# Phi exponentials kept in their attention phase, splits on GpSimd, a TensorE warm-up and a separately normalised last group in a four-segment attention and GeGLU kernel

One core of one Trainium2 chip. The metric is the device time of one execution in microseconds (us).

TensorE multiplies matrices; VectorE, ScalarE and GpSimd work element by element; DMA moves data between memories. "Half clock" means that TensorE's matmuls start half as often as they can: 0.425 us apart instead of 0.216 for 512 columns in the kernel before. "pv" is the product p @ vs; "rows" are the inverted denominators of the softmax or the memory, laid out for a matmul that spreads them.

## The reference, cut to what matters

x is 2048 x 448, bf16. It is layer-normalised once; a memory-augmented attention and a GeGLU feed-forward block both read the result, and the output is x + attention * silu(ffn).

```python
for s in range(4):                       # segments of L = 512 rows, 16 heads of 28
    p = softmax(qs @ ks.T * scale + causal_mask)
    a_dot = p @ vs
    pq = phi(qs)                         # phi(t) = t + 1 if t > 0 else exp(t)
    a_mem = (pq @ M) / (pq @ z + 1e-6)
    o = g * a_mem + (1 - g) * a_dot      # g = sigmoid(beta)
    pk = phi(ks)
    M, z = M + pk.T @ vs, z + pk.sum(0)
attn = o @ wo
ffn = (gelu(xn @ w_gate) * (xn @ w_up)) @ w_down     # 448 -> 1792 -> 448
out = x + attn * silu(ffn)
```

## The kernel before

The program is one hand-ordered stream: projections of segment 0, gate/up 0, attention 0, gate/up 1, attention 1, gate/up 2 and 3, attention 2, attention 3, the end. During attention, TensorE gets other matmuls ("filler": projections of the next segment, down projections, output projections) between the scores. During gate/up, leftovers run at numbered steps of a table. `later(n, fn)` puts work off by n ticks; one tick comes per gate/up step and per half step of attention.

The parts that matter, with cuts marked by `# ...`:

```python
pkp = pool("pkp", 2)                                  # buffers of pkT
def phi(g, nm, dst):
    # ...
    nc.scalar.activation(out=e[:], in_=dst[:, g, :], func=ACT.Exp)
    ph = pqT[s][:, g, :] if nm == "wq" else pkp.tile([P, L], BF16, name="pkT")[:]
    def rest():                                       # three VectorE operations
        # ...
        if nm == "wk":
            nc.sync.dma_start_transpose(out=pk[...], in_=ph)   # pkT -> pkb by DMA
    later(1, rest)
# after a projection of q or k:  later(2, lambda: phi(g, nm, dst))

def invert(s, side):                                  # 1/denominators as three bf16 terms
    d = dc.pop((s, side))
    # ... tensor_scalar, reciprocal on VectorE
    for i in range(3):
        nc.vector.tensor_copy(out=t[:, i, :], in_=d[:])
        if i < 2:
            nc.vector.tensor_tensor(out=d[:], in0=d[:], in1=t[:, i, :], op=ALU.subtract)
        nc.sync.dma_start(out=rows[side][...], in_=t[:, i, :])
# combine(s, g): a matmul spreads rows over group g's partitions (m<-rows,spread),
#   then VectorE multiplies and adds into oT; the output projection reads oT

# attention(s, fill): 12 steps (4 groups x 3 blocks), pv two steps behind the scores
while fill and done < 1.5:
    c, f = fill.pop(0); f(); done += c
for k, (g, bk) in enumerate(steps):
    pts[k] = scores(s, g, bk)                         # then exp on ScalarE, mask on GpSimd
    if k >= 2:
        give(k - 2)                                   # pv
    # ... filler by share of the work, tick()

# the end
for f in ends: f()                                    # the last two pv
tick()
for n, u in enumerate(d3[2:]):                        # 18 units of down projection
    run([u])
    if n == 4: invert(3, 0)
    if n >= 8 and n % 2 == 0 and n < 16: combine(3, (n - 8) // 2)
run(finish_units(3))                                  # output projection, product, store
```

## Time and profile before

| | before |
|---|---|
| time, median (lowest to highest) | 304.43 us (303.82 to 304.52) |
| span of the profiled run | 302.1 us |
| TensorE busy | 254.0 us, 84% |
| VectorE, ScalarE, GpSimd busy | 193.8, 156.6, 88.9 us |

TensorE is the bound, so its timeline is the one to cut into phases. I cut it at the first gate/up matmul of each segment, at the first V projection after gate/up 0, at the first memory read of each attention (`m<-pqT,mbd`), at the first q projection after gate/up 3, and at the end of the last output projection of attention 3; the rest is "the end".

### The profile page before, as it was taken

The page shows a single profiled execution, that of the slowest core. Times are in us where ns is not written, and L with a number is a line of the kernel's source. Part 1 is how long each engine was busy: PE and PEld are TensorE (multiplying, and loading weights), DVE is VectorE, ACT ScalarE, POOL GpSimd, SP SyncE. Part 2 cuts the span into 40 slices and gives each one's busy share as a digit, 9 for nine tenths or more (in the row PEclk, how much of TensorE's full clock was granted, in tenths as well). Part 3 has the DMA queues.
Part 4 walks back from the last instruction along what each step waited for, and adds up shares of the span by engine and source line. Part 5 has one row for each costly group of instructions (what it writes and reads, how often), then busy time and mean ns, then how long its engine had stood idle before and what let it go on. Part 6 is the DMA issues. An engine that isn't in the chain of part 4 may idle for free. (4 is left out here: it accounts for less than half of the span.)

```text
span 302.1 us, 4379 instructions
## 1 busy us (share of the span) xinstructions
PE 254.0 (84%) x1530; PEld 109.7 (36%) x1552; DVE 193.8 (64%) x409; ACT 156.6 (52%) x219; POOL 88.9 (29%) x180
## 2 busy tenths in 40 slices
PE   0497999899996895989997899999799878897690
PEld 0243444434433342534342344444333333332240
DVE  6646854547759666579786855665565739942584
ACT  2434473779992334476876233332788767580010
POOL 4100100245412000654650133020177824286000
PEclk9999999999999999799999999999999999997897
DMA  8996023001101232001110220000200001001002
GB/s 237 355 325 119 8 49 81 3 0 21 21 17 21 42 96 65 2 24 33 37 34 1 43 52 0 7 4 3 61 17 17 34 7 16 0 29 39 8 1 69
DMA packets 26358, 15.10 MB, mean 50 GB/s; under 512 B 17880, under 2 KB 25048, under 8 KB 26328
## 3 DMA queue, kind: packets, MB, share of 16 engines
q1 hardware_dynamic: 23464, 10.21, 13.9%
q10 hardware_dynamic: 2288, 3.15, 3.3%
q0 software_dynamic: 576, 1.38, 1.3%
q8 instruction: 14, 0.23, 0.3%
q14 instruction: 16, 0.13, 0.2%
HBM read 9.18 MB, written 1.84 MB: 36 GB/s over the span
## 5 line engine op out<-in xcount | busy, mean ns | idle before, releaser
L373 ACT ACTIVATE pt<-s 128x1024 bf16<-128x1024 f32 (+1 forms) x96 | 79.3, 880 | 25.5 <-PE s L367 24.0
L377 POOL TENSOR_SCALAR_AFFINE_SELECT pt<-pt 128x256 bf16<-128x256 bf16 x128 | 50.8, 417 | 102.8 <-ACT pt L373 100.5
L463 ACT ACTIVATE gl<-s 128x512 bf16<-128x512 f32 x56 | 33.2, 597 | 69.2 <-PE s L460 44.6
L464 DVE TENSOR_TENSOR hT<-gl,s 128x512 bf16<-128x512 bf16 x56 | 38.2, 686 | 39.9 <-ACT gl L463 39.8
L460 PE MATMUL s<-xnT,wg_sb 128*128 128x512 bf16 x216 | 56.9, 379 | 7.2 <-DVE hT L464 6.7
L460 PE MATMUL s<-xnT,wu_sb 128*128 128x512 bf16 x222 | 57.1, 379 | 0.1
L475 PE MATMUL m<-wd_sb,hT 128*128 128x448 bf16 x224 | 52.7, 368 | 1.1 <-DVE kT L295 0.9
L460 PEld LDWEIGHTS <-wg_sb 128*128 128x128 bf16 x224 | 21.4, 97 | 33.7 <-issue 9.5
L460 PEld LDWEIGHTS <-wu_sb 128*128 128x128 bf16 x224 | 21.9, 98 | 26.5
L475 PEld LDWEIGHTS <-hT 128*128 128x128 bf16 x224 | 21.4, 101 | 26.1 <-issue 8.9
L367 PE MATMUL s<-qT,kT 32*128 32x512 bf16 (+3 forms) x256 | 22.0, 304 | 8.0 <-ACT pt L373 7.7
L235 POOL TENSOR_TENSOR rstd<-rstd,nhalf 128x2 f32<-128x2 f32 x8 | 6.1, 757 | 52.8 <-DVE rstd L233 52.8
L478 ACT ACTIVATE th<-m 128x448 f32<-128x448 f32 x16 | 8.7, 546 | 22.0 <-PE m L475 22.0
L388 PE MATMUL pv<-pt,vaug 128*32 128x512 bf16 (+3 forms) x256 | 18.1, 308 | 2.4 <-POOL pt L377 2.1
L291 PE MATMUL m<-xnT,wq_pad 128*128 128x512 bf16 x58 | 17.7, 408 | 1.6 <-ACT xnT L250 0.7
L291 PE MATMUL m<-xnT,wk_pad 128*128 128x512 bf16 x60 | 17.1, 397 | 0.4 <-issue 0.3
L295 DVE CAST kT<-m 128x512 bf16<-128x512 f32 x16 | 11.0, 686 | 10.0 <-PE m L291 10.0
L367 PEld LDWEIGHTS <-kT 32*128 32x128 bf16 x256 | 6.9, 91 | 28.8 <-issue 28.4
L324 PE MATMUL m<-wv_sb,xnT 128*128 128x448 bf16 x64 | 14.4, 362 | 1.7 <-DVE vaug L326 1.5
L504 PE MATMUL m<-wo_sb,oT 128*128 128x448 bf16 x64 | 14.8, 354 | 0.2 <-DVE oT L449 0.2
L310 DVE TENSOR_SCALAR ph_e<-ph_e 128x512 bf16<-128x512 bf16 x24 | 12.0, 498 | 4.6 <-ACT ph_e L304 4.6
L432 PE MATMUL m<-rows,spread 128*128 128x512 bf16 x27 | 10.5, 390 | 4.9 <-DMA rows<-terms 3.7
(95 smaller groups left out, 268.4 us busy)
## 6 DMA issues: line engine op xcount, KB each, us to landing
x_sb<-in_A_x_dram SPq DMA_DIRECT2D x7, 224.0 KB
wd_sb<-in_B_w_down_dram SPq DMA_DIRECT2D x1, 1568.0 KB
wg_sb<-in_B_w_gate_dram SPq DMA_DIRECT2D x1, 1344.0 KB
wu_sb<-in_B_w_up_dram ACTq DMA_DIRECT2D x1, 1344.0 KB
out_dram<-o_out POOLq DMA_DIRECT2D x12, 112.0 KB, 2.0
xr<-in_A_x_dram ACTq DMA_DIRECT2D x2, 448.0 KB
out_dram<-o_out SPq DMA_DIRECT2D x4, 112.0 KB
wo_sb<-in_A_wo_dram SPq DMA_DIRECT2D x4, 98.0 KB
```

What stands on the lines that cost most here:

```text
L291: nc.tensor.matmul(out=pr[:], lhsT=wpad[nm][:, c, g * HG:(g + 1) * HG, :].rearrange("p h d -> p (h d)"), rhs=xnT[s][:, c, :], start=(c == ...
L310: nc.vector.tensor_scalar(out=e[:], in0=e[:], scalar1=1.0, scalar2=None, op0=ALU.min)
L324: nc.tensor.matmul(out=vp[:, 0:D], lhsT=xnT[s][:, c, b * P:(b + 1) * P], rhs=wv_sb[:, c, :], start=(c == 0), stop=(c == NDC - 1))
L367: nc.tensor.matmul(out=sp[i // 2][:, i % 2, c0:c0 + n], lhsT=kT[s][r, g, kb * P:(kb + 1) * P], rhs=qT[s][r, g, kb * P:L], start=True, stop ...
L373: nc.scalar.activation(out=pt[:, :, 0:w], in_=sp[pr][:, :, 0:w], func=ACT.Exp, scale=scale)
L377: nc.gpsimd.affine_select(out=v, in_=v, pattern=[[0, 2], [1, P]], compare_op=ALU.is_ge, fill=0.0, base=0, channel_multiplier=-1)
L388: nc.tensor.matmul(out=acc[i * HP:(i + 1) * HP, kb * P:L], lhsT=va[:, kb, g * HG + i, :], rhs=pts[i // 2][:, i % 2, c0:c0 + n], start=(kb ...
L460: nc.tensor.matmul(out=gu[:, i, :], lhsT=w_sb[:, c, fc * P:(fc + 1) * P], rhs=xnT[s][:, c, :], start=(c == 0), stop=(c == NDC - 1))
L463: nc.scalar.activation(out=gl[:], in_=gu[:, 0, :], func=ACT.Gelu_apprx_tanh)
L464: nc.vector.tensor_tensor(out=hT[s][:, fc, :], in0=gl[:], in1=gu[:, 1, :], op=ALU.mult)
L475: nc.tensor.matmul(out=d_ps[:, 0:D], lhsT=hT[s][:, fc, b * P:(b + 1) * P], rhs=wd_sb[:, fc, :], start=(fc == 0), stop=(fc == NFC - 1))
L504: nc.tensor.matmul(out=a_ps[:, 0:D], lhsT=oT[s][:, g, b * P:(b + 1) * P], rhs=wo_sb[:, g, :], start=(g == 0), stop=(g == G - 1))
```

## The change

The intent: no table loads inside gate/up (flush the waiting work when an attention ends), VectorE relieved of the splits, TensorE's clock raised before the first projections, the gap behind the first scores filled, and the last group's inverse apart, so that three groups can be combined early.

```diff
+        idle = ps_pv.tile([P, L], F32, name="pv")
+        wz = const.tile([P, P], BF16, name="wz")
+        nc.gpsimd.memset(wz[:], 0.0)
+        for i in range(100):
+            nc.tensor.matmul(out=idle[:, 0:P], lhsT=wz[:], rhs=wz[:], start=True, stop=True)
...
-        def invert(s, side):
+        def invert(s, side, g0=0, g1=G, eng=None, queues=None):
+            eng, queues = eng or nc.gpsimd, queues or [nc.sync] * 3
...
-                nc.vector.tensor_copy(out=t[:, i, :], in_=d[:])
+                eng.tensor_copy(out=t[p, i, :], in_=d)
                 if i < 2:
-                    nc.vector.tensor_tensor(out=d[:], in0=d[:], in1=t[:, i, :], op=ALU.subtract)
-                nc.sync.dma_start(
+                    eng.tensor_tensor(out=d, in0=d, in1=t[p, i, :], op=ALU.subtract)
+                queues[i].dma_start(
...
-            while fill and done < 1.5:
+            ahead(1.2)
             for k, (g, bk) in enumerate(steps):
                 pts[k] = scores(s, g, bk)
+                if k == 0:
+                    ahead(3.6)
...
+            flush()
             k = len(steps)
...
-        table = tail(0, {}, ends, 4, 8)
+        table = tail(0, {}, ends, 5, 10)
...   (the same shift of inverse and combine steps in the later phases, and of the layer-norm steps;
...    memory scalings on every second step; the multiplication behind a down projection two ticks later instead of one)
-        for f in ends:
-            f()
-        tick()
-        for n, u in enumerate(d3[2:]):
+        rest, n = d3[2:], 0
+        fast = dict(eng=nc.vector, queues=[nc.sync, nc.scalar, nc.gpsimd])
+        table = {0: [lambda: invert(3, 0, 0, G - 1)], 1: ends[:1], 3: ends[1:],
+                 8: [lambda: invert(3, 0, G - 1, G, **fast)]}
+        in_turn(table, 5, [lambda g=g: combine(3, g) for g in range(G - 1)])
+        for n, u in enumerate(rest):
             run([u])
-            if n == 4:
-                invert(3, 0)
-            if n >= 8 and n % 2 == 0 and n < 16:
-                combine(3, (n - 8) // 2)
+            for f in table.get(n, ()):
+                f()
+        flush()
+        combine(3, G - 1)
         run(finish_units(3))
```

More of the change, by code (lines that the diff above doesn't have):

```diff
@@ L181, in later, with flush @@
             waiting.append((clock[0] + n, clock[0], fn))
+        def flush():
+            while waiting:
+                tick()
         def tick():
@@ L270, in layer_norm_steps @@
             stats, scale_x, turn = layer_norm(s)
-            for n, f, b in ((0, stats, 0), (1, stats, 1), (2, stats, 2), (3, stats, 3),
-                            (3, scale_x, 0), (3, turn, 0), (4, scale_x, 1), (4, turn, 1),
-                            (7, scale_x, 2), (7, turn, 2), (8, scale_x, 3), (8, turn, 3)):
+            for n, f, b in ((0, stats, 0), (2, stats, 1), (3, stats, 2), (4, stats, 3),
+                            (5, scale_x, 0), (5, turn, 0), (6, scale_x, 1), (6, turn, 1),
+                            (8, scale_x, 2), (8, turn, 2), (9, scale_x, 3), (9, turn, 3)):
                 table.setdefault(n, []).append(lambda f=f, b=b: f(b))
@@ L412, in memory_read @@
             evac(s, g, 1, np_)
-        def invert(s, side):
-            d = dc.pop((s, side))
-            nc.vector.tensor_scalar(out=d[:], in0=d[:], scalar1=(1e-6 if side else 0.0),
-                                    scalar2=igate[:, side:side + 1], op0=ALU.add, op1=ALU.mult)
-            nc.vector.reciprocal(out=d[:], in_=d[:])
+        def invert(s, side, g0=0, g1=G, eng=None, queues=None):
+            eng, queues = eng or nc.gpsimd, queues or [nc.sync] * 3
+            p = slice(g0 * HG * RC, g1 * HG * RC)
+            d = dc[s, side][p, :]
+            nc.vector.tensor_scalar(out=d, in0=d, scalar1=(1e-6 if side else 0.0),
+                                    scalar2=igate[p, side:side + 1], op0=ALU.add, op1=ALU.mult)
+            nc.vector.reciprocal(out=d, in_=d)
             t = work.tile([P, 3, 64], BF16, name="terms")
             for i in range(3):
-                nc.vector.tensor_copy(out=t[:, i, :], in_=d[:])
+                eng.tensor_copy(out=t[p, i, :], in_=d)
                 if i < 2:
-                    nc.vector.tensor_tensor(out=d[:], in0=d[:], in1=t[:, i, :], op=ALU.subtract)
-                nc.sync.dma_start(
-                    out=rows[side][32 * i:32 * i + H, :].rearrange("h (c f) -> h c f", f=64),
-                    in_=t[:, i, :])
+                    eng.tensor_tensor(out=d, in0=d, in1=t[p, i, :], op=ALU.subtract)
+                queues[i].dma_start(
+                    out=rows[side][32 * i + g0 * HG:32 * i + g1 * HG, :].rearrange(
+                        "h (c f) -> h c f", f=64),
+                    in_=t[p, i, :])
         def inverses(side, g):
@@ L483, in rest @@
                                                    in1=d_ps[:, 0:D], op0=ALU.add, op1=ALU.mult)
-                later(1, rest)
+                later(2, rest)
                 yield
@@ L556, in give, with ahead @@
                     evac(s, g, 0, acc[g])
-            while fill and done < 1.5:
-                c, f = fill.pop(0)
-                f()
-                done += c
+            def ahead(t):
+                nonlocal done
+                while fill and done < t:
+                    c, f = fill.pop(0)
+                    f()
+                    done += c
+            ahead(1.2)
             for k, (g, bk) in enumerate(steps):
                 pts[k] = scores(s, g, bk)
+                if k == 0:
+                    ahead(3.6)
                 if k >= 2:
@@ L603, in tail, with memory @@
             return in_turn(table, n_comb, [lambda g=g: combine(s, g) for g in range(G)])
-        def memory(s, table, n_read, n_inv, n_scale):
+        def memory(s, table, n_read, n_inv, n_scale, every=1):
             in_turn(table, n_read, [lambda g=g: memory_read(s, g) for g in range(G)])
             in_turn(table, n_inv, [lambda: invert(s, 1)])
-            return in_turn(table, n_scale, [lambda g=g: scale_memory(s, g) for g in range(G)])
+            return in_turn(table, n_scale, [lambda g=g: scale_memory(s, g) for g in range(G)], every)
         table = in_turn({}, 4, [lambda: next(check)] * 5)
@@ L627, in fast_path @@
         pre = [(0.22, [lambda g=g: memory_read(1, g)]) for g in range(G)]
-        at = memory(1, {}, 99, 5, 9)
+        at = memory(1, {}, 99, 5, 10, 2)
         ends = attention(1, pre + merge([(0.9, [lambda: update(1)])], pu[8:12])
                          + merge(down_units(1), finish_units(0), pu[:8]), at)
-        table = tail(1, {}, ends, 4, 8)
+        table = tail(1, {}, ends, 5, 10)
         layer_norm_steps(3, table)
         gate_up(2, table)
-        table = memory(2, {}, 0, 6, 9)
+        table = memory(2, {}, 0, 6, 10)
         in_turn(table, 5, [lambda: update(2)])
@@ L646, in fast_path @@
         ends = attention(2, merge(pu[8:12], pu[:8], finish_units(1)) + d2[:2])
-        at = tail(2, {}, ends, 5, 9)
+        at = tail(2, {}, ends, 5, 10)
         pre = [(0.22, [lambda g=g: memory_read(3, g)]) for g in range(G)]
-        memory(3, at, 99, 6, 12)
+        memory(3, at, 99, 6, 14, 2)
         ends = attention(3, pre + d2[2:] + merge(finish_units(2), d3[:2]), at)
-        for f in ends:
-            f()
-        tick()
-        for n, u in enumerate(d3[2:]):
+        rest, n = d3[2:], 0
[4 more added lines that the diff above has]
+        for n, u in enumerate(rest):
             run([u])
-            if n == 4:
-                invert(3, 0)
-            if n >= 8 and n % 2 == 0 and n < 16:
-                combine(3, (n - 8) // 2)
+            for f in table.get(n, ()):
+                f()
+        flush()
+        combine(3, G - 1)
         run(finish_units(3))
-        tick()
-        tick()
+        flush()
         return ok
```

## The prediction

> **What bounds the kernel now.** I read the engine totals first, then TensorE's timeline for its idle gaps, then the other engines around each gap.
>
> ```profile
> PE 254.0 (84%) x1530; PEld 109.7 (36%) x1552; DVE 193.8 (64%) x409; ACT 156.6 (52%) x219; POOL 88.9 (29%) x180
> ```
>
> TensorE is the bound, with 48.1 us of the 302.1 us span not busy: 11.2 before its first instruction, 7 after its last (295.17 to 302.1), some 30 in between. The change adds no useful work; it can only win gaps and time at a low clock. The timeline has four kinds (start, length, engine, line; in brackets the idle time before and who ended it).
>
> ```profile
> 14.15 1.87 PE L291 MATMUL m<-xnT,wq_pad 128*128 128x512 bf16 x4 [0.73 <-ACT xnT L250]
> ...
> 19.80 1.03 PE L291 MATMUL m<-xnT,wq_pad 128*128 128x512 bf16 x4
> ...
> 26.17 0.43 DVE L312 TENSOR_TENSOR pkT<-ph_u,ph_e 128x512 bf16<-128x512 bf16 x1 [1.62 <-DMA pkb<-pkT]
> ...
> 27.19 0.92 PE L324 MATMUL m<-wv_sb,xnT 128*128 128x448 bf16 x4 [1.50 <-DVE vaug L326]
> ```
>
> The start. The first projections run at half rate (starts 0.425 us apart, later 0.216) until about 18.7 us. But TensorE then stops on V's PSUM buffers, because VectorE stands on a pkT buffer until a transpose DMA lands at 26.1. The DMA is fully used until then (share 0.93 to 1.31 in every microsecond from 12 to 26).
>
> ```profile
> 87.19 1.28 ACT L304 ACT_TABLE_LOAD   x1
> ...
> 89.13 1.28 ACT L463 ACT_TABLE_LOAD   x1
> ...
> 91.79 1.02 PE L460 MATMUL s<-xnT,wg_sb 128*128 128x512 bf16 x4 [1.17 <-DVE hT L464]
> ...
> 94.80 1.02 PE L460 MATMUL s<-xnT,wg_sb 128*128 128x512 bf16 x4 [1.12 <-DVE hT L464]
> ...
> 100.96 1.02 PE L460 MATMUL s<-xnT,wg_sb 128*128 128x512 bf16 x4 [0.82 <-DVE hT L464]
> ```
>
> Gate/up of segment 1. One leftover phi exponential sits between two gelus and brings a table load before and after it; the gelus stop for 2.7 us plus its own 0.63, and two stalls follow. The third stall is VectorE doing the inverse's splits (98.8 to 100.0) ahead of two hT products. Segment 2 has the same at 163.38, 166.41 and 172.56 (1.17, 1.15, 0.81).
>
> ```profile
> 120.37 0.34 PE L367 MATMUL s<-qT,kT 32*128 32x384 bf16 x2 [1.58 <-ACT pt L373]
> 121.28 0.61 PE L367 MATMUL s<-qT,kT 32*128 32x384 bf16 x6 [0.58 <-ACT pt L373]
> 121.82 1.89 PE L344 MATMUL m<-vaug,pkb 128*128 128x128 bf16 x16
> ```
>
> Every attention phase opens so: the second scores wait for the first exponentials. In segment 1 the clock falls too: the same 16 update matmuls took 1.07 us at 55.76.
>
> ```profile
> 274.98 0.75 PE L388 MATMUL pv<-pt,vaug 128*32 128x256 bf16 x4 [2.06 <-POOL pt L377]
> 275.67 6.06 PE L475 MATMUL m<-wd_sb,hT 128*128 128x448 bf16 x25
> 284.24 0.38 PE L432 MATMUL m<-rows,spread 128*128 128x512 bf16 x1 [2.52 <-DMA rows<-terms]
> 284.46 2.03 PE L475 MATMUL m<-wd_sb,hT 128*128 128x448 bf16 x6
> ```
>
> The end. Two waits, each followed by slow matmuls: six down matmuls take 2.03 us, elsewhere 1.30.
>
> **What the Trainium skill says.** "TensorE: Matmul & The Clock Gate", "What's actually happening": the array starts at half clock, is released after a busy window of about 3.4 us, and falls back after an idle one; the window runs free. The trace agrees on the rates and on roughly 4 us to recover, but a 2.06 and a 2.52 us gap with thin work around them were enough to lose the clock. "ScalarE: Activation LUTs", "What ACT_TABLE_LOAD costs": 1283 ns, the same here, plus a drain of about 1380 ns which this trace doesn't show (a gelu ends at 87.17, the load starts at 87.19, the next exponential at 88.48). "DMA: Bandwidth & Descriptors", "Queues, rings and completion order": each DMA engine takes a ring's descriptors in ring order. That fits the first pkT transpose, issued at 21.58 on the queue that carries wd and wo and landing at 26.1. "SBUF — State Buffer" says VectorE and GpSimd lock a shared port pair; here a VectorE minimum took 1.14 us instead of 0.28 beside a GpSimd addition (155.04).
>
> **The change part by part.** I compared the built instruction order of both kernels.
>
> *Warm-up, 100 matmuls of 128 columns.* Before, 16 such matmuls took 1.07 us warm (57 ns apart) and 1.89 cold (106 ns). Starting at about 1.8, with 34 to 56 of them cold, they end at 9.3 to 10.4, before the transposes at 11.2. If the clock then held, the projections would gain 8 starts at 0.425 instead of 0.216 and a little more: 2 us. But from 10 to 14.15 there are only 16 short transposes (0.9 us of warm work), thinner than the stretches that lost the clock elsewhere, so I give it 60% to be cold again at 14.15. And if it holds, V still needs the transpose DMA near 26: the 1.50 us stall becomes 3.7, and the clock is then likely lost into gate/up (about 1.7 us). Gain 0 (-2 to +1).
>
> *Exponentials flushed.* ScalarE's table loads go from 11 to 7: the two pairs at 87 and 158 vanish, 4 x 1.283 = 5.1 us of ScalarE. On the path: 1.17 + 1.12 and 1.17 + 1.15 = 4.6. Costs: the last kT exponential (0.63) now runs before the first gelu, moving it from 86.57 to about 87.2, so hT 0 is ready at 88.46; TensorE's step 2 began at 88.72. No stall. Gain 4.6.
>
> *Splits on GpSimd.* VectorE loses 3 x 0.20 + 2 x 0.24 = 1.1 us per inverse, and inverse and combination come one and two steps later. This should take the 0.82 and 0.81 at 100.96 and 172.56, and the 0.51 at 203.48. Gain 2.1. The spread-out scalings in attention 3 should take most of 0.16 + 0.88 + 0.22 near 256 to 260, and later combinations about half of the 1.15 at 254.10. Gain 1.6.
>
> *More filler behind the first scores.* The gaps are 0.36 + 0.58 (attention 0), 1.58 + 0.58 (1), 1.50 + 0.58 (2), 0.73 + 0.58 (3). They aren't all won, since the next scores need the second pair of exponentials: in attention 0 exponentials run 56.13 to 58.07 and 58.49 to 60.43, and scores 2 cannot finish before about 60.4, against 60.62 now: 0.3. Attention 1: scores 2 move from 126.15 to about 123.5, with the clock kept: 2.6. Attention 2: ScalarE has only some 2.5 us idle in the phase: 0.7. Attention 3: 1.0. Gain 4.6.
>
> *The end.* Two down units now come before the last-but-one pv and two more before the last, so those gaps (0.4 + 2.06) fill. But groups 0 to 2 split on GpSimd behind its last output addition and store, which ended at 277.13. Five operations of about 0.25 us (scaled from GpSimd's 611 and 1268 ns at 512 columns), then the 3.45 us from first issue (280.79) to landing (284.24) seen before: rows at about 280.8. TensorE arrives at about 276.7: a 4 us wait, and a cold restart. After it remain 12 down units, 34 x 0.187 + 0.6 for the spreads + 1.7 for the clock = 8.7 us, to 289.5 instead of 291.8. The last group's spread, its two VectorE operations (1.37) and four final blocks of 1.25 us on VectorE follow with nothing to cover them; before, they had overlapped. Gain 1.5.
>
> Sum: 0 + 4.6 + 2.1 + 1.6 + 4.6 + 1.5 = 14.4 us of 304.5, so 290.1; I take 290.5 for port contention.
>
> **Rivals.** *The start wins.* If the transpose lands soon after an earlier issue, the 2.2 us reach the end: 288. For it: the second transpose also landed by 26, so the first may have a microsecond in hand. Against: the DMA moves the same bytes.
>
> *The start loses.* The longer stall costs the clock when gate/up begins: 292.
>
> *GpSimd becomes the wait.* The splits stand in its strict order among the masks of pt; a split that waits for a dc transfer holds the masks and then pv. Against: pv follows its mask two steps later and GpSimd is 29% busy. With it in attention 1 and 3: 294.
>
> *The end wins as meant.* If the splits find GpSimd free and rows land near 278.5, the wait is 2 us and the clock stays: 287.
>
> *ScalarE takes over in attention.* It was 94% busy from 80 to 90, and the flush and the filler press it more: 2 to 3 us back, 293.
>
> **Range and chances.** The 4.6 of the exponentials is safest, as table loads are fixed in the program. The filler's and the splits' 8.3 could half fail; start and end could each move by 3. So 285.5 to 296. Over 2% faster needs below 298.4, some 6 us: it fails only if nearly everything but the tables fails: 0.93 faster, 0.06 same, 0.01 slower.
>
> **What would show it.** Seven table loads and none inside gate/up; gate/up of segments 1 and 2 about 26.3 us long instead of 29.4; full clock around 121. At the start, V's second part and the first gate/up matmul still near 27 and 28 us, whatever the first projections do. At the end, a wait of 3 to 5 us on rows before the first of the three spreads, then slow matmuls. I am wrong if gate/up begins before 27, if that last wait is under 2 us (better than said), or if pv waits for masks behind splits (worse).

## The result, and the profile after

300.11 us (299.60 to 301.43) against 304.43: ratio 0.9869, 95% interval 0.9835 to 0.9903. A ratio is the mean time of one kernel's fast runs over that of the other's of the same rounds, so it is not quite the ratio of the medians quoted. The kernel is faster by 1.3%, which counts as the same; 290.5 was predicted, and the range did not hold it.

Lengths of the phases in us, from the timelines of TensorE in the two profiled runs:

| phase | before | after | difference | predicted |
|---|---|---|---|---|
| start and gate/up 0 | 53.82 | 58.92 | +5.10 | 0 |
| attention 0 | 30.69 | 30.72 | +0.03 | -0.3 |
| gate/up 1 | 29.39 | 26.25 | -3.14 | -3.1 |
| attention 1 | 42.20 | 39.55 | -2.65 | -2.6 |
| gate/up 2 and 3 | 56.90 | 52.87 | -4.03 | -3.6 |
| attention 2 | 27.49 | 27.84 | +0.35 | -0.7 |
| attention 3 | 31.55 | 30.22 | -1.33 | -2.6 |
| the end, to the span's end | 30.06 | 31.73 | +1.67 | -1.5 |
| span | 302.10 | 298.10 | -4.00 | -14.4 |

The middle of the kernel did almost what was foretold. The first line and the last ate it. The totals of the page of the changed kernel answer to the line of totals shown of before:

```profile
PE 262.4 (88%) x1652; PEld 116.2 (39%) x1652; DVE 189.1 (63%) x381; ACT 151.4 (51%) x215; POOL 97.8 (33%) x217
```

TensorE is busy for 8.4 us more, 7.0 of them with warm-up matmuls. ScalarE is 5.2 us lighter, four table loads of 1.283 us.

The start, in the timeline of TensorE of the changed kernel, with one line of VectorE's timeline (L323) in its place:

```profile
1.60 7.01 PE L93 MATMUL pv<-wz 128*128 128x128 bf16 x100 [1.60 <-POOL wz L91]
...
14.17 1.87 PE L302 MATMUL m<-xnT,wq_pad 128*128 128x512 bf16 x4 [0.73 <-ACT xnT L261]
...
22.91 2.43 PE L335 MATMUL m<-wv_sb,xnT 128*128 128x448 bf16 x12
...
28.65 0.43 DVE L323 TENSOR_TENSOR pkT<-ph_u,ph_e 128x512 bf16<-128x512 bf16 x1 [4.44 <-DMA pkb<-pkT]
...
29.66 1.65 PE L335 MATMUL m<-wv_sb,xnT 128*128 128x448 bf16 x4 [4.31 <-DVE vaug L337]
31.10 1.91 PE L474 MATMUL s<-xnT,wg_sb 128*128 128x512 bf16 x4
```

The warm-up ends at 8.6. The first four projections take 1.87 us, exactly as before: the clock is lost again at 14.17. By the granted clock of this trace it fell at about 11.1, in the 2.62 us wait between the last warm-up matmul and the first transpose (11.23). The transpose lands at 28.65 instead of 26.17, V stops for 4.31 us, and the first gate/up matmuls take 1.91 us for four instead of 1.03: half clock.

Gate/up of segment 1, ScalarE's timeline of the changed kernel:

```profile
89.84 0.54 ACT L492 ACTIVATE th<-m 128x448 f32<-128x448 f32 x1 [0.53 <-PE m L489]
90.28 0.62 ACT L315 ACTIVATE ph_e<-kT 128x512 bf16<-128x512 bf16 x1
90.92 1.28 ACT L477 ACT_TABLE_LOAD   x1
92.22 0.60 ACT L477 ACTIVATE gl<-s 128x512 bf16<-128x512 f32 x1
```

The last phi exponential now comes before the only load, and TensorE has no wait on hT until a 0.28 us one at 110.06. The program has seven loads, as foretold.

The end, timeline of the changed kernel (GpSimd's first split, TensorE):

```profile
269.65 0.64 PE L399 MATMUL pv<-pt,vaug 128*32 128x256 bf16 x4 [0.59 <-POOL pt L388]
...
271.80 0.25 POOL L435 CAST terms<-dc 96x64 bf16<-96x64 f32 x1
...
276.00 0.58 PE L446 MATMUL m<-rows,spread 128*128 128x512 bf16 x1 [4.47 <-DMA rows<-terms]
276.38 1.32 PE L489 MATMUL m<-wd_sb,hT 128*128 128x448 bf16 x3
...
286.12 0.39 PE L446 MATMUL m<-rows,spread 128*128 128x512 bf16 x1 [0.73 <-DMA rows<-terms]
...
288.06 2.63 PE L518 MATMUL m<-wo_sb,oT 128*128 128x448 bf16 x13 [0.98 <-DVE oT L463]
```

The wait for masks shrank from 2.06 to 0.59, but the wait for the rows grew from 2.52 to 4.47 and is followed by half-clock matmuls (three in 1.32 us), and two more waits stand before the output projection: 0.73 for the last group's rows and 0.98 for its combination.

### The profile page after: what moved, and what is told of

Its sections match the earlier page's. It is cut to its first block, busy times and chain, and to the rows that moved or that the text cites. A ratio compares the mean times of both kernels' runs of the same rounds, so it can differ in the third digit from the quotient of the medians.

```text
span 298.1 us, 4626 instructions
## 1 busy us (share of the span) xinstructions
PE 262.4 (88%) x1652; PEld 116.2 (39%) x1652; DVE 189.1 (63%) x381; ACT 151.4 (51%) x215; POOL 97.8 (33%) x217
## 5 line engine op out<-in xcount | busy, mean ns | idle before, releaser
L474 PE MATMUL s<-xnT,wg_sb 128*128 128x512 bf16 x224 | 58.6, 385 | 0.5 <-DVE hT L478 0.5
L474 PE MATMUL s<-xnT,wu_sb 128*128 128x512 bf16 x224 | 58.4, 384 | 0.0
L489 PE MATMUL m<-wd_sb,hT 128*128 128x448 bf16 x224 | 51.7, 362 | 0.9 <-DVE oU L462 0.9
L335 PE MATMUL m<-wv_sb,xnT 128*128 128x448 bf16 x64 | 15.9, 381 | 4.7 <-DVE vaug L337 4.5
L492 ACT ACTIVATE th<-m 128x448 f32<-128x448 f32 x16 | 8.7, 547 | 21.3 <-PE m L489 16.2
L302 PE MATMUL m<-xnT,wk_pad 128*128 128x512 bf16 x64 | 17.7, 396 | 0.0
L446 PE MATMUL m<-rows,spread 128*128 128x512 bf16 x28 | 11.2, 408 | 5.4 <-DMA rows<-terms 5.2
L412 DVE COPY oU<-pv 128x512 f32<-128x512 f32 x16 | 11.0, 686 | 6.6 <-PE pv L399 6.5
```

What stands on the lines that cost most here:

```text
L302: nc.tensor.matmul(out=pr[:], lhsT=wpad[nm][:, c, g * HG:(g + 1) * HG, :].rearrange("p h d -> p (h d)"), rhs=xnT[s][:, c, :], start=(c == ...
L335: nc.tensor.matmul(out=vp[:, 0:D], lhsT=xnT[s][:, c, b * P:(b + 1) * P], rhs=wv_sb[:, c, :], start=(c == 0), stop=(c == NDC - 1))
L446: nc.tensor.matmul(out=r[:], lhsT=spread[:, g, :], rhs=rows[side][:], start=True, stop=True)
L474: nc.tensor.matmul(out=gu[:, i, :], lhsT=w_sb[:, c, fc * P:(fc + 1) * P], rhs=xnT[s][:, c, :], start=(c == 0), stop=(c == NDC - 1))
L489: nc.tensor.matmul(out=d_ps[:, 0:D], lhsT=hT[s][:, fc, b * P:(b + 1) * P], rhs=wd_sb[:, fc, :], start=(fc == 0), stop=(fc == NFC - 1))
```

## The experiments

Fifteen kernels ran, all with correct results. "Start" is the time of the first gate/up matmul; "to att 0" is start plus gate/up 0; "end" is from the end of the last output projection of attention 3 to the span's end. All three are from each run's profile. "Times" are the lowest to highest of the runs; "ratio" is to the kernel before in the same rounds. A star marks a line whose median and times hold runs classed slow: one each in nofill_again (299.13) and best (292.73), two in after_oldtail (298.40, 297.60). The medians of their fast runs are 296.89, 288.11 and 294.10.

| run | median, us | times | ratio | start | to att 0 | end |
|---|---|---|---|---|---|---|
| nofill | 296.29 | 294.58-296.65 | 0.968 | 28.81 | 56.13 | 31.57 |
| before_fill | 307.23 | 306.72-307.53 | 1.006 | 30.34 | 56.93 | 29.98 |
| after_pk0 | 292.95 | 291.60-293.98 | 0.958 | 26.49 | 52.37 | 32.25 |
| nofill_pk0 | 292.19 | 291.86-292.26 | 0.957 | 25.47 | 51.35 | 31.75 |
| after_again | 298.05 | 297.24-298.85 | 0.978 | 29.36 | 56.50 | 31.76 |
| nofill_again * | 297.21 | 294.65-299.13 | 0.973 | 31.94 | 58.63 | 31.79 |
| hold_pk0 | 290.82 | 290.34-294.17 | 0.957 | 24.82 | 50.70 | 31.60 |
| tailvec_pk0 | 291.86 | 290.26-293.81 | 0.957 | 27.30 | 52.97 | 30.20 |
| oldtail_pk0 | 290.88 | 288.71-292.08 | 0.958 | 25.81 | 51.48 | 28.52 |
| noflush_pk0 | 297.47 | 296.78-298.33 | 0.978 | 26.92 | 52.59 | 31.57 |
| oldfill_pk0 | 296.37 | 295.68-296.93 | 0.976 | 25.90 | 51.57 | 31.60 |
| vecsplit_pk0 | 292.72 | 292.59-293.67 | 0.964 | 26.90 | 52.57 | 29.72 |
| before_pk0 | 301.33 | 297.89-301.76 | 0.985 | 25.99 | 51.66 | 28.43 |
| after_oldtail * | 295.23 | 292.58-298.40 | 0.964 | 29.01 | 56.58 | 28.48 |
| best * | 288.16 | 287.75-292.73 | 0.946 | 24.36 | 50.24 | 28.85 |

Read the phases before the times. The start doesn't repeat, and a time holds everything. Gate/up 2 and 3 repeats to 0.02 us and gate/up 1 to 0.5 where their steps are the same. Attention 1, 2 and 3 have two lengths each, and the granted clock of the traces tells them apart: in 21 of these 51 phases it falls to half, each time for one stretch of 3.4 us. The lengths in us over the seventeen profiles, by filler and by clock:

| | clock kept | one stretch at half clock |
|---|---|---|
| attention 1, old filler | none | 42.08 to 42.57 |
| attention 1, new filler | 39.55 (nine profiles) | 40.30 to 40.34 (four) |
| attention 2, old filler | 27.49 | 28.53 to 28.74 |
| attention 2, new filler | 26.85 | 27.54 to 27.84 |
| attention 3, old filler | 31.55 (30.38 in oldfill_pk0) | 31.80 |
| attention 3, new filler | 30.22 | 31.60 to 31.72 |

So a phase must be compared at the same clock. In attention 2 the kernel before kept it and the changed kernel lost it: the +0.35 above is this draw.

### The start: nofill, before_fill, after_pk0, nofill_pk0

My theory after the result: the warm-up delays the start. Rival: the landing of the transpose varies by itself. nofill takes the warm-up out of the changed kernel, before_fill puts it into the kernel before.

```diff
-        for i in range(100):
-            nc.tensor.matmul(out=idle[:, 0:P], lhsT=wz[:], rhs=wz[:], start=True, stop=True)
```

> The changed kernel without the 100 warm-up matmuls. Theory A (the warm-up is what made the start 5.1 us later): V restarts near 27.2, gate/up of segment 0 starts near 28.2 at full clock, and the time falls from 300.1 to 295 (294.5 to 296). Rival B (the pkT transpose landed at 28.65 instead of 26.17 for a reason of its own, such as the DMA's order in that run; the warm-up is innocent): the stall stays about 4.3 us and the time stays near 300.

> The kernel before plus only the 100 warm-up matmuls. Theory A: VectorE waits some 4.4 us for the pkT transpose instead of 1.62, the clock falls to half when gate/up begins, and the time rises from 304.4 to about 309 (308 to 310). Rival B: 304.4 within 0.7, the wait still about 1.6.

nofill fell to 296.29, but on this chip the kernel before itself ran between 302.85 and 307.20, and before_fill's 307.23 is only 0.6% above it, with an interval over 1 (0.9984 to 1.0136). In before_fill's profile the landing was 27.88 and V waited 3.48. In nofill's the landing was 26.79, V waited 2.40, and the first gate/up matmuls ran at half clock even so. VectorE in nofill:

```profile
26.79 0.42 DVE L318 TENSOR_TENSOR pkT<-ph_u,ph_e 128x512 bf16<-128x512 bf16 x1 [2.53 <-DMA pkb<-pkT]
```

So a wait longer than before's and a cold gate/up don't need the warm-up. Neither theory came out as written.

after_pk0 and nofill_pk0 take away what makes VectorE wait: segment 0 writes its four pkT groups into a tile that is free at that time.

```diff
                 pqT[s] = seg1.tile([P, G, L], BF16, name="pqT")
+            else:
+                pk0 = seg1.tile([P, G, L], BF16, name="pqT")
...
-                ph = pqT[s][:, g, :] if nm == "wq" else pkp.tile([P, L], BF16, name="pkT")[:]
+                if s == 0:
+                    ph = pk0[:, g, :]
+                else:
+                    ph = pqT[s][:, g, :] if nm == "wq" else pkp.tile([P, L], BF16, name="pkT")[:]
```

> The changed kernel, warm-up kept, but segment 0 writes its four pkT groups to a tile that is free then (pqT), so VectorE never waits for a transpose to release a pkT buffer. If the loss at the start runs through that wait: V goes on without a stop after 22.9, gate/up starts near 26 at full clock instead of 31.1 at half clock, time about 293 (292 to 294.5). If the wait is not what matters (weights of gate/up or the DMA hold TensorE anyway): gate/up still starts near 30 and the time stays over 297.

> The same without the warm-up. It tells what the warm-up is worth once nothing stands behind it. In the changed kernel the projections were at half clock again by 14.17 and finished 0.34 us earlier than before; so I expect 293.3, 0.3 us more than with the warm-up. If the warm-up were worth the 2 us it was meant for, this run is 2 us slower than the one with it.

Both expectations about the wait held: V runs its 16 matmuls without a stop and gate/up starts at full clock, 26.49 with the warm-up and 25.47 without. That the version without it would be 0.3 us slower did not come: it is 0.8 us faster by the medians, with overlapping intervals. TensorE in nofill_pk0:

```profile
22.37 3.26 PE L335 MATMUL m<-wv_sb,xnT 128*128 128x448 bf16 x16
25.47 1.03 PE L474 MATMUL s<-xnT,wg_sb 128*128 128x512 bf16 x4
```

Over all seventeen profiles (the kernel before, the changed kernel and the fifteen runs), "to att 0" is 53.8 to 58.9 where VectorE waits for the transpose and 50.2 to 53.0 where it doesn't. The loss at the start goes through that wait. What spread is left without it has another source: gate/up starts between 25.47 and 27.30 in the eight profiles that have no wait and no long warm-up, according to when the clock rises (the projections run at full pace from 17.2 us in nofill_pk0, from 20.5 in tailvec_pk0).

### The warm-up again, and a longer one: after_again, nofill_again, hold_pk0

> The changed kernel once more, unaltered, beside its version without the warm-up in the same rounds. In the traces so far the transpose that VectorE waits for landed at 26.17 (before), 26.79 (no warm-up), 27.88 (before plus warm-up) and 28.65 (changed): it is a lottery, perhaps loaded by the warm-up. Expected 300, spread over 2 us.

> Theory A (the warm-up delays the start): 3 to 5 us less than the changed kernel in the same rounds, landing near 26.5. Rival B (the landing varies by itself): within 1 us of it, with as wide a spread.

In the same rounds the medians are 298.05 with and 297.21 without, 296.89 without the slow run; the ratios, 0.978 and 0.973, have intervals that overlap (0.9749 to 0.9816, 0.9685 to 0.9768). Theory A foretold 3 to 5 us and falls in that size. The fast runs differ by 1.2 us in their medians and 1.5 in their means, so the rival's "within 1 us" doesn't quite hold either. nofill_again's profile, which fell in the run classed slow and so proves no difference of times, shows a late landing with no warm-up in the program:

```profile
29.06 0.42 DVE L318 TENSOR_TENSOR pkT<-ph_u,ph_e 128x512 bf16<-128x512 bf16 x1 [5.35 <-DMA pkb<-pkT]
```

Landings with the pkT wait and a warm-up: 28.65, 27.88, 27.16, 27.24; without: 26.17, 26.79, and 29.06 in the slow run. Among the fast profiles every landing with a warm-up is later than both without; six landings in random order fall so once in fifteen times. That the landing varies by itself is seen; that the warm-up adds a microsecond or so is neither shown nor excluded.

hold_pk0 gives the warm-up what it lacked:

```diff
-        for i in range(100):
-            nc.tensor.matmul(out=idle[:, 0:P], lhsT=wz[:], rhs=wz[:], start=True, stop=True)
+        def keep_busy(n):
+            for i in range(n):
+                nc.tensor.matmul(out=idle[:, 0:P], lhsT=wz[:], rhs=wz[:], start=True, stop=True)
+        keep_busy(145)
...
                 nc.scalar.copy(out=dst, in_=tp[:])          # after each block's transposes
+                keep_busy(8)
```

> Warm-up that is long enough: 145 matmuls, then 8 after each block's transposes, over the version whose VectorE doesn't wait for pkT buffers. If the warm-up failed because TensorE fell back to half clock in the gap from 8.6 to 14.2: the projections now run at full clock from 14.2, gate/up starts near 23.4 instead of 25.5, time 290.2. If the projections are held by something else (weights landing, PSUM copies): gate/up stays near 25.5, time 292.

TensorE in hold_pk0:

```profile
1.60 10.31 PE L94 MATMUL pv<-wz 128*128 128x128 bf16 x145 [1.60 <-POOL wz L91]
...
14.82 1.02 PE L308 MATMUL m<-xnT,wq_pad 128*128 128x512 bf16 x3 [0.23 <-ACT xnT L264]
15.68 1.03 PE L308 MATMUL m<-xnT,wk_pad 128*128 128x512 bf16 x4
```

The first projections run at full clock (1.03 us for four). The fillers pushed the first projection from 14.16 to 14.8 or a little before it, and gate/up started at 24.82, not at the 23.4 expected. Against nofill_pk0's 25.47, the earliest of the eight starts without the wait and without a long warm-up, that is a gain of 0.65; against the latest, 2.5. The times don't show it: both kernels have a ratio of 0.957. Two of hold_pk0's six runs took 293.67 and 294.17, at a mean granted clock of 0.969 and 0.968 where the others had 0.975 or 0.976. The clock that fell between 8.6 and 14.2 in the changed kernel holds here, so that gap is why the 100 matmuls did next to nothing.

### The end: tailvec_pk0, oldtail_pk0, after_oldtail

```diff
-        table = {0: [lambda: invert(3, 0, 0, G - 1)],
+        table = {0: [lambda: invert(3, 0, 0, G - 1, eng=nc.vector)],
```

> No warm-up, free pkT tile, and at the end the first three groups' splits on VectorE instead of GpSimd. If the 4.47 us wait comes from the splits standing behind GpSimd's output additions and stores (they started 2.8 us after the reciprocal was done): rows land some 2.5 us earlier, the wait falls to about 2, and the time from 292.2 to about 289.5. If the wait is set by the row DMAs themselves, the time stays at 292.

The wait for the rows fell from 4.47 to 2.45, and the end from 31.75 to 30.20, 1.5 us. TensorE in tailvec_pk0:

```profile
268.01 0.38 PE L446 MATMUL m<-rows,spread 128*128 128x512 bf16 x1 [2.45 <-DMA rows<-terms]
```

A little under half of the wait was GpSimd's. What makes the rest isn't shown by a run of its own; in the trace the rows land 4.7 us after their first issue (263.33), and one split on VectorE took 1.29 us instead of 0.19 beside a GpSimd addition (263.75). The time doesn't show the gain: 291.86 against nofill_pk0's 292.19, equal ratios, where 289.5 was expected. Its profile has the latest start without the wait, 27.30.

```diff
-        rest, n = d3[2:], 0
-        ...                                             # the whole new end
+        for f in ends: f()
+        tick()
+        for n, u in enumerate(d3[2:]):
+            run([u])
+            if n == 4: invert(3, 0, eng=nc.vector)
+            if n >= 8 and n % 2 == 0 and n < 16: combine(3, (n - 8) // 2)
+        run(finish_units(3)); tick(); tick()
```

> No warm-up, free pkT tile, and the end as in the kernel before (all four groups inverted together, splits on VectorE). Phase lengths from the traces so far: from the last attention's end to the span's end 30.0 us before, 31.7 in the changed kernel, 30.2 with the splits on VectorE. If apart-normalising the last group is itself a loss, this end is 30.0 and the run 1.7 us faster than the changed end, so 290.4 against 292.2; if the old end was the slower one, the end grows over 31.7.

The end is 28.52, 3.2 us shorter than the changed one. TensorE in oldtail_pk0:

```profile
261.75 0.64 PE L399 MATMUL pv<-pt,vaug 128*32 128x256 bf16 x4 [2.04 <-POOL pt L388]
262.32 6.59 PE L489 MATMUL m<-wd_sb,hT 128*128 128x448 bf16 x25
...
270.67 0.38 PE L446 MATMUL m<-rows,spread 128*128 128x512 bf16 x1 [1.76 <-DMA rows<-terms]
270.88 1.30 PE L489 MATMUL m<-wd_sb,hT 128*128 128x448 bf16 x6
...
276.26 3.57 PE L518 MATMUL m<-wo_sb,oT 128*128 128x448 bf16 x16
```

The 2.04 us wait for masks that the change was to fill is back, and costs the clock (25 down matmuls in 6.59 us); the end is shorter all the same: the rows wait is 1.76, the clock survives it (six matmuls in 1.30 us), and no wait stands before the output projection. The old end has two lengths: 30.06 and 29.98 in before and before_fill, where the granted clock falls after both waits, 6.8 us at half clock together, and 28.43 to 28.85 in four others, where it falls once, for 3.4 us. In before_pk0 the same wait for masks left the clock alone, and its 2.40 us wait for rows didn't:

```profile
274.51 0.64 PE L393 MATMUL pv<-pt,vaug 128*32 128x256 bf16 x4 [2.06 <-POOL pt L382]
275.08 4.90 PE L480 MATMUL m<-wd_sb,hT 128*128 128x448 bf16 x25
```

The new end is 31.57 to 32.25 in every profile that has it whole, all of them with 6.8 us at half clock from the long rows wait on. Against the old end with as much half clock it is 1.5 to 2.3 us longer, against the others 2.7 to 3.8.

> The changed kernel with warm-up and pkT wait, but the end as before (one inverse for all groups, splits on VectorE). From the phases of oldtail_pk0 (28.5 us against 31.7): end 28.5 to 29.5 and 2.5 to 3.2 us less than the changed kernel, so 295 to 297.5 where the changed kernel had 298 to 300. If the end's gain belonged to the other base: 298 or more.

The same in the changed kernel itself: end 28.48, ratio 0.964 (the changed kernel had 0.987 and 0.978 in other rounds). The fast runs lie between 292.58 and 296.09, partly under what was expected. So the changed end costs 1.7 to 3.2 us, by the clock that the old end drew.

### The parts that gained: noflush_pk0, vecsplit_pk0, oldfill_pk0

All three are judged by phases against nofill_pk0 (gate/up 1 25.80, attention 1 39.55, gate/up 2 and 3 52.86).

```diff
-            flush()
             k = len(steps)
```

> The same base without the flush after each attention, so the last phi exponentials go into gate/up again. Theory: four table loads come back, gate/up of segment 1 lasts about 28.1 instead of 25.8 and that of 2 and 3 about 55.2 instead of 52.9, time 4.6 us more, 296.8. Rival (the other shifts of steps already took these stalls away): under 1.5 us more.

Gate/up 1 took 27.46 and gate/up 2 and 3 54.26: 1.7 and 1.4 more. The loads are back, ScalarE in noflush_pk0:

```profile
85.99 1.28 ACT L312 ACT_TABLE_LOAD   x1
87.28 0.63 ACT L312 ACTIVATE ph_e<-kT 128x512 bf16<-128x512 bf16 x1
87.93 1.28 ACT L477 ACT_TABLE_LOAD   x1
```

but of the pair of stalls the second is nearly gone (1.17 and 0.17 instead of 1.17 and 1.12), presumably because the layer-norm steps and the work behind it now come later; no run tests that alone. So in gate/up the flush itself is worth some 3.1 us, between the theory's 4.6 and the rival's 1.5. The run's 5 us in time hold other phases too (attention 1 took 40.33 and attention 3 31.72 there, each with a stretch at half clock that nofill_pk0 didn't have), and I don't count them.

```diff
-            eng, queues = eng or nc.gpsimd, queues or [nc.sync] * 3
+            eng, queues = eng or nc.vector, queues or [nc.sync] * 3
```

> The same base with every split on VectorE as before, at the changed steps. Theory (it is the later steps, not GpSimd, that took the gate/up stalls of 0.8, 0.8 and 0.5): gate/up 25.8 and 52.9 as with GpSimd, and the end 1.5 us shorter: 290.7. Rival (VectorE's 1.1 us per inverse was the stall): gate/up phases grow by some 0.8 each, time 292 or more.

The rival held. Gate/up 1 took 26.77 and gate/up 2 and 3 54.50: 1.0 and 1.6 more. The stalls of before return with the same lengths, TensorE in vecsplit_pk0:

```profile
98.85 1.02 PE L474 MATMUL s<-xnT,wg_sb 128*128 128x512 bf16 x4 [0.81 <-DVE hT L478]
...
165.44 1.02 PE L474 MATMUL s<-xnT,wg_sb 128*128 128x512 bf16 x4 [0.81 <-DVE hT L478]
...
194.63 1.02 PE L474 MATMUL s<-xnT,wg_sb 128*128 128x512 bf16 x4 [0.51 <-DVE hT L478]
```

GpSimd is right for the splits in gate/up and wrong for them at the end, where vecsplit_pk0 is 2.0 us shorter. In the time the two nearly cancel: 292.72 against 292.19.

```diff
-            ahead(1.2)
+            ahead(1.5)
...
-                if k == 0:
-                    ahead(3.6)
```

> The same base with the old order of filler in attention (1.5 ahead, none behind the first scores). Theory: attention 1 goes from 39.6 to about 42.2, attention 0 and 2 stay within 0.4 (ScalarE holds the second scores either way), attention 3 grows by 1: 3.5 us more, 295.7. Rival (filler only moves the gap everywhere): within 1 us.

The sum came as the theory had it, its parts only for attention 0 and 1: attention 1 42.57 (3.0 more), attention 0 30.69, attention 2 28.53 (0.7 more, at half clock in both), attention 3 30.38 (0.2 more, where 1 was expected). In attention 1 part of it is the clock, which nofill_pk0 kept. The 16 update matmuls in oldfill_pk0, then in nofill_pk0, each a line of TensorE's timeline:

```profile
116.14 1.81 PE L355 MATMUL m<-vaug,pkb 128*128 128x128 bf16 x16
```

```profile
112.98 1.06 PE L355 MATMUL m<-vaug,pkb 128*128 128x128 bf16 x16
```

The new filler doesn't always keep it, as in best:

```profile
112.91 1.68 PE L364 MATMUL m<-vaug,pkb 128*128 128x128 bf16 x16
```

Where it is lost with both fillers, the new one gains 1.7 to 2.3 us (42.08 to 42.57 against 40.30 to 40.34).

### Closing: before_pk0 and best

> The kernel before, with only the free pkT tile for segment 0. If its start carries the same lottery as the changed kernel's: V doesn't stop, gate/up starts at 25.5 to 27.3 instead of 28.2 or later, and the time is about 302 with a spread under 1.5 us, while the kernel before spreads over 3 us or more beside it. If the wait costs the kernel before nothing but the 1.5 us of its profile: 303 and both equally tight.

The kernel before gains 1.5% from the free tile alone (ratio 0.9854, 0.9799 to 0.9910). In the same rounds it ran between 302.57 and 306.73; before_pk0 had five of six runs between 301.18 and 301.76, and one of 297.89, which missed the spread that was expected; its mean granted clock is 0.993, where the other five have 0.972 to 0.983. The kernel before carries the lottery as well, and its profiled run, 53.82 us to attention 0, drew the shortest start of the seven that have the wait (the others take 56.1 to 58.9).

best joins the free tile, the long warm-up and the old end to the rest of the change:

> Free pkT tile, long warm-up, the old end with VectorE's splits, everything else as changed. From the phases: start 24.8, gate/up and attentions as in the runs so far, end 28.5: span 286, time 287.5 (286.5 to 290).

Median 288.16 us, ratio 0.9458 (0.9405 to 0.9511): the best of all. One fast run took 290.19, and a run classed slow 292.73.

## Why the prediction was wrong

**The start (0 predicted, 5.1 lost).** Three of its statements held: the clock was lost again before 14.17 (by 11.1, in the wait after a warm-up that ended at 8.6 instead of 9.3 to 10.4), V needed the transpose whatever the projections did, and a longer stall took the clock into gate/up. The step that failed is "V still needs the transpose DMA near 26": I read one run's landing as fixed by the amount of data, and took the start of before as a baseline. It landed at 28.65. The 5.1 us are 2.5 from the landing (V's second part at 29.66 instead of 27.19), 0.5 from four slow V matmuls and 2.2 from gate/up at half clock (27.82 against 25.66). I allowed 1.7 for the last, and only where the first projections had been warm. The rival "the start loses" had this path, but put the loss at some 1.5 us. Part of the 5.1 is the luck of the draw: before's start was the shortest of seven. The warm-up is not shown to be the cause: in the same rounds it costs 1.2 to 1.5 us in fast runs, with overlapping intervals. The signs of being wrong looked only for an earlier gate/up (it began at 31.10), a shorter rows wait or masks held by splits; none of them came.

**The end (1.5 gained predicted, 1.7 lost).** The wait was foretold as about 4 us with a cold restart, and was 4.47. The step that failed is the sum after it: "to 289.5 instead of 291.8", with the last group "with nothing to cover them". Both terms of it were mis-sized. From the start of the end to the last down projection I counted 2.3 us won; it was 0.7 (19.0 us instead of 19.7), since the rows wait was longer and 6.8 us passed at half clock. For the exposed chain of the last group I counted 0.8 lost; it was 2.4 (12.7 us instead of 10.3), with waits of 0.73 for its rows and 0.98 for its combination. oldtail_pk0 and after_oldtail show that the whole new order is the loss, with 1.5 us of it GpSimd's in tailvec_pk0.

**Attention 0, 2 and 3 (3.6 predicted, 1.0 gained).** ScalarE as the next limit was named. The gap moved from the second to the third scores: in attention 2 the waits are 1.07 and 0.63 in the changed kernel, where before they were 1.50 and 0.58 one step earlier:

```profile
214.09 0.28 PE L378 MATMUL s<-qT,kT 32*128 32x256 bf16 x2 [1.07 <-ACT pt L384]
```

Attention 0 gained nothing: 30.69 to 30.73 in every profile. In attention 2 the 0.7 predicted was right, 0.64 where both keep the clock (27.49 and 26.85); the changed kernel's profile lost it there. The miss is attention 3: the waits are 1.19 and 0.63, and oldfill_pk0 gives the filler 0.2 of the 1.0 that I had counted; a wait of 0.95 remains at 254.77.

**Gate/up and attention 1 (9.3 predicted, 9.8 gained)** came as worked out, in sum, which is partly luck. Within gate/up the flush was given 4.6 and measures 3.1 alone; the splits were given 2.1 and measure 2.6 alone; the two don't simply add. In attention 1 the clock was kept, as foretold; four of thirteen profiles with the new filler lost it.

**The chances.** 0.93 for faster by over 2% treated start and end as small independent errors, 3 us each; they missed by 5.1 and 3.2, both to the worse. The start alone moves "to att 0" by 5 us from profile to profile.

**Open.** What moves the landing from 26.2 to 28.7 us (29.1 in the run classed slow) I don't know: in the traces of the kernel before and of the changed kernel the DMA was full until about 25. Whether the warm-up shifts it by a microsecond or so can't be told from these runs. What decides in which attention phase the clock falls isn't shown either.

## What to carry to other kernels

Before warming TensorE's clock, follow its next instructions to the point where something else stops it, and keep it warm over the whole gap; here one buffer's release by a transpose DMA decided the start, and a free tile was worth more than the warm-up. A split-off last piece needs work to hide its whole chain (DMA, reciprocal, splits, DMA, spread, multiply, add); taken out of a loop that covered it, it shows. Profile the baseline more than once and cut the timeline into phases: the ones that repeat carry the argument, the ones that don't can't be predicted from one trace. Check the granted clock of both profiles before you read a difference of 1 us in a phase.

## What the Trainium skill lacked or had wrong

- "TensorE: Matmul & The Clock Gate", "What's actually happening", ties the fall back to one idle window of about 3.4 us. Here shorter waits were enough, and not each time: of the old end's six waits for masks, 2.04 to 2.06 us long, five were followed by half clock and one (before_pk0) by full clock; the waits for rows of 2.40 to 2.52 us cost the clock in three profiles, those of 1.76 (oldtail_pk0) and 2.21 us (best) didn't: six down matmuls in 1.30 us.
- The same section doesn't say how busy TensorE must be to keep the clock. In the changed kernel it fell at about 11.1 us, in a wait of 2.62 us; 145 matmuls and 8 after each block's transposes kept it to the projections (hold_pk0). Whether fewer would do wasn't tried.
- No page that I read says that the profile's granted clock can read full before the first change is recorded: in before it is 1.00 from 14 to 18 us while matmuls start 0.425 us apart; in the changed kernel, at the same pace, it is 0.51. "TensorE: Matmul & The Clock Gate", "Seeing it yourself", warns only in general that clock events in traces can be unreliable.
- "ScalarE: Activation LUTs", "What ACT_TABLE_LOAD costs", adds a drain of about 1380 ns to each load. The 1283 ns agree; the drain isn't seen: the load at 90.92 ends at 92.20 and the gelu starts at 92.22.
- "DMA: Bandwidth & Descriptors", "DMA Transpose (X-bar)", gives no spread of landings. The first transpose, issued at about 21.3 to 21.7, landed between 26.17 and 28.65 in fast runs under a full DMA load.
